# Gathers of an expert's rows issued inside the loop over experts, in three buffers, in place of all in one row before it

## The chip, the cores and the metric

One core of a Trainium2 chip runs the whole program. The metric is device time in microseconds (us) of that core. The engines are TensorE (PE, with its weight loads shown apart as PEld), VectorE (DVE), ScalarE (ACT), GpSimd (POOL) and SyncE (SP); SP issues most DMAs, POOL issues the indirect ones.

## The reference

Linear attention without a softmax, then a mixture of experts in which each token goes to one expert, or to none. There are 8 batches of 576 tokens, 8 heads of 64, so 4608 rows of 512; 8 experts with 512x1024 and 1024x512 weights, all in float32.

```python
kv = einsum('bhsd,bhse->bhde', k, v);  o = einsum('bhsd,bhde->bhse', q, kv)
x = (o / sqrt(mean(o * o, -1) + 1e-6) * g_norm)      # -> (4608, 512)
out = x.copy();  do = x @ w_skip > 0;  xc = x[do]
logits = xc @ w_gate;  e = argmax(logits, 1);  gate = softmax(logits)[e]
for j in range(8):
    rows = (e == j)
    y[rows] = gate[rows] * (relu(xc[rows] @ w1[j]) @ w2[j])
out[do] = xc + y
```

## The kernel before, in words

The first part (to about 142 us of the span) computes attention unit by unit, stores every normalised row x to the output tensor in HBM, and works out for each token its expert and its place within that expert. Experts are taken in the order of how many tokens they have; the r-th of them has room for `CAPS[r]` rows (line 73: 352, 352, 320, 288, 288, 288, 256, 256).

The second part takes the experts one after the other. The rows of an expert are fetched from the output tensor by indirect DMAs on POOL (`gather_piece`, L865, instructions at L868): a "piece" of 128 rows with the index table `src`, and the rest of 64 or 32 rows cut into half or quarter rows, so that 128 partitions are used, with the table `asrc`. An expert has two to four pieces. They lie in a tile `xg`; the tile of expert 0 is `xg0`, and its first piece is fetched early (L682), while attention still runs. `expert_in` (L872) turns a piece with PE transposes (L878) and DVE copies (L881, L883) into `xt`. `layer_1` (L893) makes eight groups of matmuls into PSUM tiles `hps` (L897), each followed by a Relu on ACT (L899) into `ht`; there are three `hps` buffers. `layer_2` (L901) makes the matmuls of one piece into `yps` (L908). `result` (L913) multiplies by the gate and adds x on DVE (L919, in place in `xg`), and scatters the rows back with an indirect DMA on POOL (L922).

The order is written out by hand. Ahead of the loop, `gather_all` (L934, called at L979) issues the 23 pieces that are left, expert 0 first, back to back on POOL. Then come the start of the weights of experts 1 and 2 on SP (`load_ahead`, L980), the sums for the gates, and the second layer of expert 0's first piece. The loop over experts (`experts`, L942) then does for expert r: weights of expert r+2 on SP (L262, L265), `layer_1` of r, `expert_in` of r+1, and for each piece of r `layer_2` and `result`. For expert 0 `first_tables` (L986) runs first: it splits `layer_1` in two halves of four `hps` groups, and after each half PE adds 18 small matmuls for the gates (`place`, L576), whose operand `bv` DVE makes (L567) in one buffer, so that the second `bv` waits until PE has read the first.

```python
for r in range(E):                        # gather_all, L934
    for piece in pieces[r]:
        gather_piece(xgs[r], piece, src, asrc)
```

Gathers read the output tensor and scatters write it. The scheduling layer knows that no two scatters meet, but between a gather and a scatter it puts a wait for whichever stands first in the program. The pools of the second part lie one behind the other in SBUF, over the tiles of the attention part: weights, gathered rows (`gather`), `ffn` (`xt`, `ht`) and `slot` (tables).

After the loop the kernel computes whether any expert had more rows than its room, and repeats the second part in a loop that is not entered with these inputs.

Of the kernel before, what the change touches and what calls it, by code (L numbers as in the profile page):

```python
# [8 lines left out]
FP32 = mybir.dt.float32  # L9
# [8 lines left out]
def kernel(  # L18
# [37 lines left out]
    DM = H * D  # L56
    N = B * S
    P = 128
# [6 lines left out]
    E, F = moe_w1.shape[0], moe_w1.shape[2]  # L65
# [8 lines left out]
    CK = CAP // 128  # L74
# [135 lines left out]
    for a in range(2):  # L210
        r = slice(a * 64, (a + 1) * 64)
# [47 lines left out]
    def load_weights(r, pool):  # L259
        e = experts_of[r]  # L260
        w1 = pool.tile([P, DC, F], FP32, tag="w1", name="w1")
        nc.sync.dma_start(out=w1[:, :, :],  # L262
                          in_=moe_w1[bass.ds(e, 1)].rearrange("o (c p) f -> p (o c) f", p=P))
        w2 = pool.tile([P, FC, DM], FP32, tag="w2", name="w2")
        nc.sync.dma_start(out=w2[:, :, :],  # L265
                          in_=moe_w2[bass.ds(e, 1)].rearrange("o (c p) d -> p (o c) d", p=P))
        w_sb[r] = (w1, w2)
# [385 lines left out]
    xg0 = keep.tile([P, CK, DM], FP32)  # L653
# [120 lines left out]
    with tc.tile_pool(name="wpool_b", bufs=2, reuse_waits="tile") as wpool_b, \  # L774
# [69 lines left out]
        def plan_of(r):  # L844
            pieces = [(c * P, P, r * CK + c) for c in range(CAPS[r] // P)]
            i = 0
            for (_, m), rs in kinds.items():
                for j, (r_, off) in enumerate(rs):
                    if r_ == r:
                        pieces.append((off, m, i + j))  # L850
                i += len(rs)
            return pieces

        plan = [plan_of(r) for r in range(E)]
        whole = [[(c * P, P, r * CK + c) for c in range(CK)] for r in range(E)]
# [9 lines left out]
        def gather_piece(xg, piece, src, asrc):  # L865
            off, m, col = piece
            idx = src if m == P else asrc
            nc.gpsimd.indirect_dma_start(  # L868
                out=x_of(xg, off, m), out_offset=None, in_=cut_rows(m)[:, :],
                in_offset=bass.IndirectOffsetOnAxis(ap=idx[:, col:col + 1], axis=0))  # L870
# [16 lines left out]
        def new_xt():  # L887
            return ffn.tile([P, DC, CAP], FP32, tag="xt", name="xt")

        def new_ht():  # L890
            return ffn.tile([P, FC, CAP], FP32, tag="ht", name="ht")

        def layer_1(r, xt, ht, cols, fs):  # L893
            for f in fs:
                hps = ps_h.tile([P, CAP], FP32, tag="hps", name="hps")
                for dc in range(DC):
                    nc.tensor.matmul(out=hps[:, cols], lhsT=w_sb[r][0][:, dc, f * P:(f + 1) * P],  # L897
                                     rhs=xt[:, dc, cols], start=(dc == 0), stop=(dc == DC - 1))
                nc.scalar.activation(out=ht[:, f, cols], in_=hps[:, cols], func=ACT.Relu)  # L899

        def layer_2(r, ht, piece):  # L901

            off, m, _ = piece
            n = DM * m // P
            yps = ps_y.tile([P, DM], FP32, tag="yps", name="yps")
            for f in range(FC):
                for q in range(P // m):
                    nc.tensor.matmul(out=yps[q * m:(q + 1) * m, 0:n], lhsT=ht[:, f, off:off + m],  # L908
                                     rhs=w_sb[r][1][:, f, q * n:(q + 1) * n],
                                     start=(f == 0), stop=(f == FC - 1), skip_group_check=True)  # L910
            return yps

        def result(piece, yps, xg, tables, group):  # L913

            off, m, col = piece
            n = DM * m // P
            rows, gate = tables[0 if m == P else 1]
            x = x_of(xg, off, m)
            nc.vector.scalar_tensor_tensor(  # L919
                out=x, in0=yps[:, 0:n], scalar=gate[:, col:col + 1], in1=x,  # L920
                op0=ALU.mult, op1=ALU.add)
            ins = nc.gpsimd.indirect_dma_start(  # L922
                out=cut_rows(m)[:, :],
                out_offset=bass.IndirectOffsetOnAxis(ap=rows[:, col:col + 1], axis=0),
                in_=x, in_offset=None, bounds_check=N * P // m - 1, oob_is_err=False)
            tc.declare_no_dep(ins.ins, group=group, reason="each row has one slot")
            tc.add_to_no_dep_group(group, ins.ins)

        def load_ahead(r):
            for ahead in (r, r + 1, r + 2):  # L930
                if ahead < E and ahead not in w_sb:
                    load_weights(ahead, wpool_b if ahead % 3 else wpool_a)

        def gather_all(pieces, src, asrc):  # L934
            xgs = [xg0] + [gather_pool.tile([P, CK, DM], FP32, tag="xg", name="xg", bufs=E - 1)
                           for _ in range(E - 1)]
            for r in range(E):
                for piece in pieces[r]:
                    gather_piece(xgs[r], piece, src, asrc)
            return xgs  # L940

        def experts(pieces, xgs, xt, ht, yps0, tables, group):  # L942

            for r in range(E):
                load_ahead(r)
                todo = pieces[r]
                end = todo[-1][0] + todo[-1][1]
                if r == 0 and yps0 is not None:
                    tables = first_tables(lambda fs: layer_1(r, xt, ht, slice(P, end), fs), tables)
                    result((0, P, 0), yps0, xgs[0], tables, group)  # L950
                else:
                    layer_1(r, xt, ht, slice(0, end), range(FC))
                if r + 1 < E:
                    xt = new_xt()
                    for piece in pieces[r + 1]:
                        expert_in(xgs[r + 1], xt, piece)
                for piece in todo:
                    result(piece, layer_2(r, ht, piece), xgs[r], tables, group)
                del w_sb[r]
                ht = new_ht()  # L960

        first = (0, P, 0)
        assert plan[0][0] == first
        plan[0] = plan[0][1:]
        xt0, ht0 = new_xt(), new_ht()
# [10 lines left out]
        settle(NE, NT, bv)  # L976
        rows, src = slot_rows(slice(0, NCOL), slot_pool, "")
        arows, asrc = again_rows()
        xgs = gather_all(plan, src, asrc)  # L979
        load_ahead(0)  # L980
        gates()
        yps0 = layer_2(0, ht0, first)
# [3 lines left out]
        def first_tables(layer, tables):  # L986

            gp = g_ps[:, GB:GB + 3 * NCOL]
            half = NT // 2
            for i, t in enumerate((0, half)):  # L990
                bv = columns(t, half, colid_i, gate_k, 3, slot_pool, half)
                layer(range(i * FC // 2, (i + 1) * FC // 2))
                place(gp, bv, t, half, t == 0, t == half)
            gate = slot_gates_of(gp)
            agate = slot_pool.tile([P, NRES], FP32, tag="agate", name="agate")
            nc.vector.tensor_copy(out=agate[:, :], in_=again_of(gate))
            return (tables[0], gate), (tables[1], agate)
        experts(plan, xgs, xt0, ht0, yps0, (rows, arows), "first")


        over = slot_pool.tile([P, E, E], FP32)
# [11 lines left out]
        more = slot_pool.tile([P, ROUNDS], FP32)  # L1013
# [10 lines left out]
        with tc.For_i(1, n_rounds, 1):  # L1024
            nc.vector.tensor_single_scalar(out=colid[:, :], in_=colid[:, :], scalar=CK, op=ALU.add)
            nc.vector.tensor_single_scalar(out=number_f[:, :], in_=number_f[:, :],
                                           scalar=float(CAP), op=ALU.add)
            nc.vector.memset(srow[:, :], 0.0)
            add_pieces(srow[:, :], place_all(colid, row_k, 2), 2)

            left = slot_pool.tile([P, NCOL], FP32, tag="left", name="left")
            nc.vector.tensor_tensor(
                out=left[:, :].rearrange("p (r c) -> p r c", c=CK),
                in0=number_f[:, :].unsqueeze(1).to_broadcast([P, E, CK]),
                in1=caps[:, :].unsqueeze(2).to_broadcast([P, E, CK]), op=ALU.is_ge)
            nc.vector.tensor_tensor(out=srow[:, :], in0=srow[:, :], in1=left[:, :], op=ALU.mult)
            rows, src = slot_rows(slice(0, NCOL), slot_pool, "")
            xgs = gather_all(whole, src, None)
            gate = slot_gates(colid)
            xt0 = new_xt()  # L1040
            for piece in whole[0]:
                expert_in(xg0, xt0, piece)
            experts(whole, xgs, xt0, new_ht(), None, ((rows, gate), None), "more")


# [26 lines left out]
```

## Time and profile before

| what | us |
|---|---|
| median of 3 runs | 457.79 |
| lowest and highest run | 456.39, 461.09 |
| the profiled execution | 460.54 |
| its span, first to last instruction | 458.8 |
| mean granted TensorE clock in the span | 0.931 |

All rows are of the one profiled execution; their times count from the start of its span. In a timeline or chain a row gives start, duration and what ran, and in square brackets how long the engine was idle just before and what ended that. "issue" as the releaser means that the profile shows nothing that the engine waited for. In a table by windows each row is one stretch; PEclk is the granted TensorE clock as a share of its upper level of 2.4 GHz, DMA the mean busy share of the 16 DMA engines (overlapping packets can take it over 1), GB/s what they moved.

### The profile page before, as it was taken

The numbers are of one execution on the slowest core, as the hardware profiler recorded it, in microseconds if no ns is written. First come the engines' busy times: TensorE is split into PE (matmuls) and PEld (weight loads), VectorE is DVE, ScalarE is ACT, GpSimd is POOL, SyncE is SP. The second block draws the span as 40 slices with busy tenths as digits, with TensorE's granted clock in tenths as the row PEclk, the third lists the DMA queues.
The fourth block names the chain that finished last, engine by engine and source line by source line (L and its number), as shares of the span: only waits on it lengthen the run. The fifth ranks groups of instructions, "written<-read, shape, count | busy, mean of one in ns | idle before, by whom it ended". The sixth has DMA issues, their size and how long they took to land.

```text
span 458.8 us, 8810 instructions
## 1 busy us (share of the span) xinstructions
PE 389.5 (85%) x3777; PEld 271.7 (59%) x3777; DVE 128.6 (28%) x316; ACT 96.3 (21%) x236; POOL 116.0 (25%) x185
## 2 busy tenths in 40 slices
PE   0699997797655983689999999999999999999980
PEld 0588886676544862455654764674764865856730
DVE  3125566577997630121011010110010011010010
ACT  1156674464531300100210110110110110201100
POOL 2016665545466277102001100100100101001010
PEclk9999998988865997589999999999999999999996
DMA  7999999952379999251541614524623600001000
GB/s 234 332 390 390 397 401 324 338 166 55 94 246 366 356 390 316 85 207 44 179 161 45 221 21 186 161 72 191 193 80 141 211 0 24 25 1 46 0 23 21
DMA packets 32779, 81.82 MB, mean 178 GB/s; under 512 B 3326, under 2 KB 3330, under 8 KB 32736
## 3 DMA queue, kind: packets, MB, share of 16 engines
q1 hardware_dynamic: 26656, 66.59, 41.2%
q0 software_dynamic: 4576, 14.54, 9.0%
q8 instruction: 31, 0.51, 0.5%
q10 hardware_dynamic: 1504, 0.08, 0.2%
q14 instruction: 12, 0.10, 0.1%
HBM read 66.87 MB, written 14.61 MB: 178 GB/s over the span
## 4 chain that ended last, share of the span: by engine, by line
PE 76%; DVE 8%; DMA 7%; issue 5%; ACT 1%; POOL 0%; DVEq 0%; ACTq 0%; POOLq 0%
PE hps L897 30%; PE yps L908 27%; PE o_ps L393 5%; PE sum_ps L291 4%; PE q_ps L353 3%; DMA q<-in_q_dram 2%; DVE xl L422 2%; PE xp L878 2%; DMA xg<-out_dram,src 2%; DMA wraw<-in_moe_w_gate_dram 1%; DMA xg<-out_dram,asrc 1%; PE g_ps L320 1%; DVE oha_k L550 1%; DVE xt L881 1%; DVE rs L405 1%
## 5 line engine op out<-in xcount | busy, mean ns | idle before, releaser
L897 PE MATMUL hps<-xt,w 128*128 128x288 f32 (+5 forms) x576 | 138.4, 400 | 8.4 <-issue 7.6
L908 PE MATMUL yps<-w,ht 128*32 128x128 f32 (+2 forms) x672 | 132.9, 413 | 0.0
L897 PEld LDWEIGHTS hps<-xt,w 128*128 128x128 f32 x576 | 107.7, 198 | 37.9 <-issue 11.9
L908 PEld LDWEIGHTS yps<-w,ht 128*32 128x32 f32 (+2 forms) x672 | 63.8, 145 | 66.1 <-issue 63.1
L899 ACT ACTIVATE ht<-hps 128x288 f32<-128x288 f32 (+5 forms) x72 | 28.3, 393 | 261.1 <-PE hps L897 234.8
L922 POOL DMA_INDIRECT out_dram<-xg,rows x16 | 15.8, 988 | 225.3 <-DVE xg L919 219.4
L919 DVE SCALAR_TENSOR_TENSOR xg<-yps,gate,xg 128x512 f32<-128x512 f32 x16 | 12.0, 751 | 108.5 <-PE yps L908 108.5
L393 PE MATMUL o_ps<-kvn,qT 64*64 64x73 f32 (+1 forms) x384 | 34.1, 271 | 6.5 <-DVE xl L422 5.9
L291 PE MATMUL sum_ps<-v,k 64*64 64x64 f32 x1152 | 26.8, 251 | 14.8 <-DMA v<-in_v_dram 10.5
L881 DVE COPY xt<-xp 128x512 f32<-128x512 f32 x16 | 10.4, 686 | 101.4 <-PE xp L878 97.4
L455 POOL TENSOR_TENSOR xb<-xl,g_b 128x512 f32<-128x512 f32 x32 | 38.3, 1198 | 0.0
L393 PEld LDWEIGHTS o_ps<-kvn,qT 64*64 64x64 f32 (+1 forms) x384 | 28.6, 173 | 14.0 <-DVE xl L422 7.3
L291 PEld LDWEIGHTS sum_ps<-v,k 64*64 64x64 f32 x1152 | 23.7, 162 | 18.1 <-issue 17.3
L393 PE MATMUL o_ps<-kvs,qT 64*64 64x73 f32 (+1 forms) x384 | 33.4, 272 | 0.9 <-issue 0.9
L405 DVE TENSOR_REDUCE rs<-sq 128x8 f32<-128x512 f32 x36 | 24.5, 679 | 16.4 <-ACT sq L397 15.9
L422 DVE TENSOR_TENSOR xl<-o_ps,rs 128x584 f32<-128x584 f32 x36 | 27.6, 767 | 4.7 <-DVE rs L419 0.5
L393 PEld LDWEIGHTS o_ps<-kvs,qT 64*64 64x64 f32 (+1 forms) x384 | 27.9, 173 | 0.4 <-ACT rs L412 0.4
L439 POOL TENSOR_TENSOR lp<-xl 128x36 f32<-128x36 f32 x36 | 9.2, 255 | 68.9 <-DVE xl L422 68.7
L353 PE MATMUL q_ps<-ident,q 128*128 128x128 f32 x128 | 23.4, 312 | 2.8 <-DMA q<-in_q_dram 2.8
L356 ACT COPY qT<-q_ps 128x512 f32<-128x512 f32 x32 | 18.8, 587 | 30.2 <-PE q_ps L353 30.0
L397 ACT ACTIVATE sq<-o_ps 128x512 f32<-128x512 f32 x36 | 21.5, 597 | 15.8 <-PE o_ps L393 15.6
L353 PEld LDWEIGHTS q_ps<-ident,q 128*128 128x128 f32 x128 | 16.2, 157 | 5.6 <-DMA q<-in_q_dram 3.2
(146 smaller groups left out, 243.0 us busy)
## 6 DMA issues: line engine op xcount, KB each, us to landing
w<-in_moe_w_dram SPq DMA_DIRECT2D x16, 2048.0 KB, 8.9
k<-in_k_dram SPq DMA_DIRECT2D x8, 1152.0 KB, 13.1
v<-in_v_dram SPq DMA_DIRECT2D x8, 1152.0 KB, 14.9
q<-in_q_dram SPq DMA_DIRECT2D x8, 1152.0 KB, 13.2
out_dram<-xb SPq DMA_DIRECT2D x8, 512.0 KB, 10.4
out_dram<-xb POOLq DMA_DIRECT2D x8, 512.0 KB
out_dram<-x SPq DMA_DIRECT2D x2, 256.0 KB, 7.9
out_dram<-x POOLq DMA_DIRECT2D x2, 256.0 KB
```

What stands on the lines that cost most here:

```text
L291: nc.tensor.matmul(out=sum_ps[w * 64:(w + 1) * 64, a, u, :], lhsT=kt[r, 2 * u + w, c, :], rhs=vt[r, 2 * u + w, c, :], start=(c == 0), stop ...
L353: nc.tensor.transpose(out=ps[:, w, :, hf, :], in_=qts[b][:, 2 * u + w, c:c + 2, :], identity=ident[:, :])
L356: nc.scalar.copy(out=qT[:, :, :, :].rearrange("p w a t -> p (w a t)"), in_=ps[:, :, :, :, :].rearrange("p w a h t -> p (w a h t)"))
L393: nc.tensor.matmul(out=ps[to, r, cols], lhsT=lhsT, rhs=kv[rows, u, a * KD:(a + 1) * KD], start=True, stop=True, skip_group_check=True)
L397: nc.scalar.activation(out=sq[:, :, :, :], in_=heads(ps, G, G + 2 * D), func=ACT.Square)
L405: nc.vector.tensor_reduce(out=rs[:, :, :], in_=sq[:, :, :, :].rearrange("p r w (a d) -> p r (w a) d", a=2), axis=AX.X, op=ALU.add)
L422: nc.vector.tensor_tensor(out=xl[:, :, :, :].rearrange("p r w (a k) -> p r (w a) k", a=2), in0=ps[:, :, 0:2 * PK].rearrange("p r (h k) -> ...
L455: nc.gpsimd.tensor_tensor(out=xb[:, :, 4 * u * D:(4 * u + 4) * D].rearrange("p r (w x) -> p r w x", w=2), in0=xl[:, :, :, G:G + 2 * D], in ...
L897: nc.tensor.matmul(out=hps[:, cols], lhsT=w_sb[r][0][:, dc, f * P:(f + 1) * P], rhs=xt[:, dc, cols], start=(dc == 0), stop=(dc == DC - 1))
L899: nc.scalar.activation(out=ht[:, f, cols], in_=hps[:, cols], func=ACT.Relu)
L908: nc.tensor.matmul(out=yps[q * m:(q + 1) * m, 0:n], lhsT=ht[:, f, off:off + m], rhs=w_sb[r][1][:, f, q * n:(q + 1) * n], start=(f == 0), s ...
L922: ins = nc.gpsimd.indirect_dma_start(out=cut_rows(m)[:, :], out_offset=bass.IndirectOffsetOnAxis(ap=rows[:, col:col + 1], axis=0), in_=x, ...
```

## The change

`gather_all` now issues the pieces of one expert. Ahead of the loop it is called for experts 0 and 1; in the loop, at the start of the turn of expert r (from r = 1 on), for expert r+1. The tiles of experts 1 to 7 share three buffers in place of seven of their own. The pool is so smaller by four tiles of 3 x 512 floats in each partition (24 KB), and the pools `ffn` and `slot` behind it lie that much lower.

```diff
-        def gather_all(pieces, src, asrc):
-            xgs = [xg0] + [gather_pool.tile([P, CK, DM], FP32, tag="xg", name="xg", bufs=E - 1)
-                           for _ in range(E - 1)]
-            for r in range(E):
+        xgs = {}
+
+        def gather_all(r, pieces, src, asrc):
+            if r < E:
+                xgs[r] = xg0 if r == 0 else gather_pool.tile([P, CK, DM], FP32, tag="xg", name="xg",
+                                                             bufs=3)
                 for piece in pieces[r]:
                     gather_piece(xgs[r], piece, src, asrc)
-            return xgs
...
             for r in range(E):
                 load_ahead(r)
+                if r:
+                    gather_all(r + 1, pieces, *srcs)
                 todo = pieces[r]
...
         arows, asrc = again_rows()
-        xgs = gather_all(plan, src, asrc)
+        for r in range(2):
+            gather_all(r, plan, src, asrc)
         load_ahead(0)
```

On POOL, behind the last gather of expert 1 (its quarter-row piece) and ahead of the first scatter; `xg_211` is the tile of expert 0, and a row "x2" stands for two instructions:

```order
 L868 DMA xg<-out_dram,asrc 128x128
-L868 DMA xg<-out_dram,src 128x512 x2
-L868 DMA xg<-out_dram,asrc 128x256
-L868 DMA xg<-out_dram,src 128x512 x2
-L868 DMA xg<-out_dram,asrc 128x128
-L868 DMA xg<-out_dram,src 128x512 x2
-L868 DMA xg<-out_dram,asrc 128x128
-L868 DMA xg<-out_dram,src 128x512 x2
-L868 DMA xg<-out_dram,asrc 128x128
-L868 DMA xg<-out_dram,src 128x512 x4
 L922 DMA out_dram<-xg_211,rows 4608x512 x2
```

The sixteen gathers of experts 2 to 7 are gone from here (twelve of 128x512, one of 128x256, three of 128x128 floats); seven gathers stay ahead of the first scatter.

On POOL in the changed kernel, from the last scatter of expert 0 to the gathers for expert 3, with what each instruction waits for; `DMASW` names are the semaphores of POOL's DMAs, eight in turn:

```order
L922 DMA out_dram<-xg_211,arows 18432x128 [waits DVE_49]
L868 DMA xg<-out_dram,src 128x512 [waits DMASW6_49,DMASW7_49,DMASW5_49,DMAHW2_49,DMASW4_49,PE_49]
L868 DMA xg<-out_dram,src 128x512
L868 DMA xg<-out_dram,asrc 128x256
L922 DMA out_dram<-xg,rows 4608x512 [waits DMASW1_49,DMASW2_49,DMASW0_49,DVE_49]
L922 DMA out_dram<-xg,rows 4608x512 [waits DVE_49]
L922 DMA out_dram<-xg,arows 9216x256 [waits DVE_49]
L922 DMA out_dram<-xg,arows 18432x128 [waits DVE_49]
L868 DMA xg<-out_dram,src 128x512 [waits DMASW5_49,DMASW6_49,DMASW4_49,DMASW3_49]
L868 DMA xg<-out_dram,src 128x512
L868 DMA xg<-out_dram,asrc 128x128
```

The gathers for an expert now stand behind the scatters of the expert two before it, and the first of them waits until those scatters have landed; the first scatter of the next expert waits until these gathers have landed. PE, DVE, ACT and SP keep the order of their instructions.

## Rows read from the trace of the kernel before

**Rows 1.** The page, busy time, share of the span and instructions of each engine.

```profile
PE 389.5 (85%) x3777; PEld 271.7 (59%) x3777; DVE 128.6 (28%) x316; ACT 96.3 (21%) x236; POOL 116.0 (25%) x185
```

**Rows 2.** The chain that ended last: start us, us, what.

```profile
167.10 6.32 PE hps L897 x32
173.42 0.60 PE g_ps L576 x14
...
174.73 1.93 issue
...
179.47 0.22 PE g_ps L576
...
189.35 0.53 PE hps L897
...
197.16 0.60 PE g_ps L576 x18
...
199.40 0.75 DVE xg L919
...
201.88 13.59 PE yps L908 x112
...
340.39 0.45 PE xp L878 x4
```

**Rows 3.** ACT in order of time, the first three hps groups of expert 0.

```profile
168.92 0.36 ACT L899 ACTIVATE ht<-hps 128x224 f32<-128x224 f32 x1 [10.76 <-PE hps L897]
174.56 0.36 ACT L899 ACTIVATE ht<-hps 128x224 f32<-128x224 f32 x1 [5.28 <-issue]
188.66 0.36 ACT L899 ACTIVATE ht<-hps 128x224 f32<-128x224 f32 x1 [13.75 <-issue]
```

**Rows 4.** DVE in order of time, the second operand for the gates.

```profile
190.32 1.51 DVE L567 TENSOR_TENSOR bv<-ohc,gate_k 128x1296 bf16<-128x1296 bf16 x1 [20.55 <-remote]
```

**Rows 5.** Windows: us, each engine's busy time and instructions, PEclk, DMA share, GB/s.

```profile
160.00:175.00 15.00, 12.89 (x65) 9.29 (x64) 4.92 (x10) 0.72 (x2) 11.50 (x12) 1.00 1.04 389
175.00:180.00 5.00, 0.63 (x3) 0.20 (x2) 0.00 (x0) 0.00 (x0) 3.78 (x4) 0.69 0.99 352
180.00:185.00 5.00, 1.06 (x2) 0.86 (x3) 0.00 (x0) 0.00 (x0) 3.78 (x4) 0.50 0.66 198
185.00:190.00 5.00, 2.13 (x4) 0.86 (x3) 0.00 (x0) 0.36 (x1) 0.95 (x1) 0.50 0.45 144
...
188.50:190.00 1.50, 0.53 (x1) 0.29 (x1) 0.00 (x0) 0.36 (x1) 0.00 (x0) 0.50 0.00 0
...
200.00:205.00 5.00, 4.40 (x10) 1.96 (x9) 2.02 (x5) 0.00 (x0) 1.03 (x1) 0.66 1.01 379
```

**Rows 6.** POOL's gathers and scatters in order of time.

```profile
157.48 1.03 POOL L868 DMA_INDIRECT xg<-out_dram,src  x1 [11.35 <-DVE src L648]
...
166.35 0.94 POOL L868 DMA_INDIRECT xg<-out_dram,src  x1 [0.30 <-issue]
...
185.25 0.95 POOL L868 DMA_INDIRECT xg<-out_dram,src  x1 [0.31 <-issue]
...
244.19 0.98 POOL L922 DMA_INDIRECT out_dram<-xg,rows  x1 [26.63 <-DVE xg L919]
...
256.58 0.98 POOL L922 DMA_INDIRECT out_dram<-xg,arows  x1 [1.20 <-DVE xg L919]
```

**Rows 7.** The chain, what ended the wait for expert 0's last gathered piece.

```profile
160.11 6.12 DMA xg<-out_dram,asrc
```

**Rows 8.** Windows behind the last scatters of experts 1 and 3.

```profile
264.10:272.90 8.80, 8.80 (x35) 6.19 (x34) 0.00 (x0) 1.75 (x4) 0.00 (x0) 1.00 0.00 0
...
325.00:334.60 9.60, 9.60 (x41) 7.55 (x40) 0.35 (x1) 1.64 (x4) 0.98 (x1) 1.00 0.77 249
334.60:340.30 5.70, 5.70 (x25) 4.39 (x25) 0.00 (x0) 1.23 (x3) 0.00 (x0) 1.00 0.00 0
```

**Rows 9.** The page's DMA queues: packets, MB, share of 16 engines.

```profile
q8 instruction: 31, 0.51, 0.5%
```

More of the change, by code (lines that the diff above doesn't have):

```diff
@@ L932, in load_ahead, with experts @@
                     load_weights(ahead, wpool_b if ahead % 3 else wpool_a)
-        def gather_all(pieces, src, asrc):
-            xgs = [xg0] + [gather_pool.tile([P, CK, DM], FP32, tag="xg", name="xg", bufs=E - 1)
-                           for _ in range(E - 1)]
-            for r in range(E):
+        xgs = {}
[3 more added lines that the diff above has]
+                                                             bufs=3)
                 for piece in pieces[r]:
                     gather_piece(xgs[r], piece, src, asrc)
-            return xgs
-        def experts(pieces, xgs, xt, ht, yps0, tables, group):
+        def experts(pieces, srcs, xt, ht, yps0, tables, group):
             for r in range(E):
                 load_ahead(r)
+                if r:
+                    gather_all(r + 1, pieces, *srcs)
                 todo = pieces[r]
@@ L997, in first_tables @@
             return (tables[0], gate), (tables[1], agate)
-        experts(plan, xgs, xt0, ht0, yps0, (rows, arows), "first")
+        experts(plan, (src, asrc), xt0, ht0, yps0, (rows, arows), "first")
         over = slot_pool.tile([P, E, E], FP32)
@@ L1037 @@
             rows, src = slot_rows(slice(0, NCOL), slot_pool, "")
-            xgs = gather_all(whole, src, None)
+            for r in range(2):
+                gather_all(r, whole, src, None)
             gate = slot_gates(colid)
@@ L1042 @@
                 expert_in(xg0, xt0, piece)
-            experts(whole, xgs, xt0, new_ht(), None, ((rows, gate), None), "more")
+            experts(whole, (src, None), xt0, new_ht(), None, ((rows, gate), None), "more")
 _INS = ['q', 'k', 'v', 'g_norm', 'moe_w_skip', 'moe_w_gate', 'moe_w1', 'moe_w2']
```

## The prediction, made before the changed kernel had run

> **What bounds the kernel now.** I read the page first, then the chain of waits in order of time, then ACT, DVE and POOL around the one place where the chain is not PE's own work, and last windows over that place. The page says that PE works for 389.5 us, 85% of the span of 458.8 [rows 1]. So most of the time is matmuls that the change does not touch, and the reader should look for the stretch in which PE does nothing. The chain shows it: after the first half of expert 0's layer 1 (167.10, 6.32 us for 32 records) and 14 of the 18 small gate matmuls, PE goes over to single instructions with gaps of 1 to 2 us put down to "issue", that is, to nothing that the profile shows, and it returns to its usual pace only behind the matmul at 189.35 [rows 2]. From 199.40, when DVE takes the result of expert 0's first piece, the chain is PE's layers up to the end.
>
> I call that stretch the trickle, and these signs go with it. ACT, which waits for nothing but PE there, takes the second hps group at 174.56 and the third at 188.66, though PE had run all four groups by 173.42 [rows 2, 3]. DVE makes the second gate operand at 190.32, over 10 us after the last of the 18 matmuls for which it waits, which ran at 179.47 [rows 2, 4]. So not only are PE's next instructions late, also what PE has done is learnt late by others. The windows tell what runs meanwhile: from 175 to 190 PE is busy for 0.63, 1.06 and 2.13 us of 5, and the granted clock falls to 0.50 [rows 5]. All that time POOL's train of 23 gathers is under way: first at 157.48, then one each 1.25 us, last at 185.25 [rows 6]. In the window 188.50 to 190.00 the DMA engines are quiet (0 GB/s) [rows 5], and just there ACT, PE and DVE come free. I read it so: the trickle belongs to the gathers in flight. It is not plain DMA load: from 160 to 175 the engines moved 389 GB/s at a share of 1.04 and PE was busy for 12.89 us of 15, while from 185 to 190 the share was 0.45 and PE still trickled [rows 5]. Which part of the chip holds PE up I can't read from the trace; that is the weak point of the forecast.
>
> **The change part by part.** Seven gathers stay ahead of the loop (three for expert 0, four for expert 1), the first at 157.48; the row at 166.35 is the first of the sixteen that move [rows 6]. PE ran at its usual pace until 173.4, with ten or more gathers issued [rows 2, 6]. So with seven I expect no trickle.
>
> First term, the trickle. In the traced run 199.40 - 173.42 = 25.98 us pass from the gate matmuls of the first half to DVE's result. Without the trickle this stretch holds: the 18 gate matmuls, 0.60 x 18/14 = 0.77 us; the second half of layer 1, the same work as the first half, 6.32 us; and from 197.16 to 199.40 what stands there now, 2.24 us. Sum 9.33 us [rows 2]. DVE's second operand (1.51 us) lies beside the second half and stays hidden [rows 4]. Gain 25.98 - 9.33 = 16.65 us.
>
> Second term, the clock. The idle PE left the granted clock at 0.66 in the window 200 to 205 [rows 5]. Layer 2 of expert 0's remaining pieces (128, 64 and 32 rows) took 13.59 us [rows 2]; the same three kinds of piece of expert 1 took 256.58 - 244.19 = 12.39 us from scatter to scatter [rows 6]. Gain 1.20 us.
>
> Third term, the sixteen gathers in the loop. POOL's own time there is free: after the train it only scatters, and three issues at 1.25 us, 3.75 us a turn, lie beside PE's layers. What can cost is a gather that lands late, because PE's transposes of expert r+1 stand ahead of layer 2 of r in PE's queue, and everything waits behind them. The chain of a gather is now: last scatter of the expert two before, its landing, two or three issues at 1.25 us, the landing of the last. For the tightest case, r = 4: nothing moves any more from 334.60 on, so the scatters of expert 3 have landed by then [rows 8]; three gathers need 2.5 us to the start of the last and, as the end of the train shows (185.25 to 188.50), at most 3.25 us more [rows 5, 6]. That makes 340.35, and PE wants the rows at 340.39 [rows 2]. So it just fits with the latest landing, and has room if the scatter lands before the load of weights beside it has ended. For r = 2 the quiet begins at 264.10 [rows 8], and with 5.75 us more the rows are there at 269.85, 3 us before the transposes at 272.90. The upper bound is a train of three as it went beside full load, from 157.48 to 160.11 + 6.12 = 166.23, 8.75 us [rows 6, 7]: then r = 4 is 3.0 us late, and r = 2 comes at 272.85, just in time. Doubling the 3.0 for the turns whose rows I don't show, the bounds of this term are 0 and some 6 us of loss; a gain is excluded, since no gather is waited for in the loop now. I take 0.5 us, near the quiet rows, because the loads of weights end before the gathers can begin. A rule speaks against the move: the Trainium skill, page "DMA: Bandwidth & Descriptors", section "Issuing engines are not separate DMA queues", says that transfers issued by different engines share the same 16 DMA engines and interleave, so that a gather on POOL's queue gets no way past the weights on SP's. By it the sum would be the 6 us of loss if both ran together; by the quiet row at 334.60 they hardly meet.
>
> The waits that the lower place of the `xt`, `ht` and table tiles changes concern tiles of the attention part, which ended at 142 us or so; I cost them at nothing, covered by PE's work, and at most at the 1 us that one ACT start could move.
>
> Sum: 16.65 + 1.20 - 0.5 = 17.35 us off the profiled execution's 460.54, which makes 443.2. That execution lies 2.75 us over the median of the three runs, 457.79; taken off the median it would be 440.4. I take 442, about between the two.
>
> **The rivals.** Shorter, not gone: what starves is each engine's fetch of its own instructions, which has to pass the same DMA engines, and the trickle ends when they have room. Then the gain is the bytes that leave the stretch: twelve times 256 KB, once 128 and three times 64 KB, 3.47 MB, at the 389 GB/s of the full stretch 8.9 us [rows 5]. Time 460.54 - 8.9 = 451.6, near 450 against the median. The Trainium skill, page "Runtime: NRT & Kernel Launch", section "Instruction fetch mechanics", says that each sequencer fetches its next block of 16 KiB by a DMA queue of its own while it executes the current one; the trace agrees with 31 packets and 0.51 MB on that queue [rows 9]. For it speaks "issue" as the releaser; against it that the trickle went on at a DMA share of 0.45, and that ACT and DVE were late in seeing PE's finished work, which no fetch of PE explains.
>
> Not touched: the trickle comes from the seven gathers together with the 8 MB of weights of experts 1 and 2, which stay. Then POOL's queue is shorter and nothing else changes: 458. For it speaks that the weights are under way in the first half of the trickle; against it the trickle's last 5 us with a low DMA share, and PE's full pace while the first gathers flew.
>
> Slower: the trickle goes with gathers wherever they are. Then 16.65 us for 23 gathers, or 1.04 each if only the sixteen late ones made it, come back in the loop, where PE is never idle: 16 x 1.04 = 16.7 us, and each of six trains drops the clock for once 1.2 us, 7.2 together. Total 460.54 - 17.85 + 16.7 + 7.2 = 466.6. It is slower than before from (17.85 - 7.2)/16 = 0.67 us a gather. Against it stands that PE ran at pace beside the first nine or ten.
>
> **How the numbers follow.** Trickle gone, 436 to 448 (the two bases, 4 us below for a clock that stays up, the late gathers' 6 us above): 0.58. Shorter, about 450: 0.16. Untouched, about 458: 0.15. Slower, about 466: 0.11. The range runs from 436 up to 458, which leaves out the slow case and half of the untouched one. About 1%, 4.6 us, is what a measurement of this kernel can tell from no change: the first two cases are faster by more, which makes 0.73 with a little taken off for late gathers; the untouched case is the same, 0.16; the last is slower, 0.11.
>
> **What would show it.** Right: on PE no gaps of 1 to 2 us put down to "issue" behind the first half of layer 1; ACT's third hps start some 1.5 us after its second; DVE's result of expert 0's first piece near 183 in place of 199.40; a granted clock that stays at 1.0 (the upper level, 2.4 GHz) from there on; in the loop PE's transposes without a wait for a gather. Wrong: gaps of that kind that last until about 181 (the second case) or 190 (the third), or that turn up behind each train in the loop (the fourth); a wait of PE's transposes for `src` or `asrc` gathers of 2 us and more in several turns would show the third term too small.

## The result, and the profile after

The changed kernel takes 442.53 us (median of 4 runs, 442.13 to 443.48), beside 457.09 us for the kernel before in the same runs (4 runs, 455.11 to 461.09). The ratio is 0.9674, with a 95% interval of 0.9605 to 0.9743: 3.3% faster. (Here and below, medians and ranges are of all runs, while ratios leave out runs that took over 1.5% longer than the fastest of the same kernel.) The profiled execution of the changed kernel took 442.29 us with a span of 440.5 us, 18.3 us less than the span before. So the run fell where the likeliest case had it, 0.5 us from the predicted 442. What the experiments add is that the kernel before does not always show the trickle; where it doesn't, it is as fast as the changed kernel is elsewhere, and there is nothing for the change to take away.

The page of the changed kernel, busy time of each engine (compare [rows 1]):

```profile
PE 381.5 (87%) x3777; PEld 266.7 (61%) x3777; DVE 127.4 (29%) x316; ACT 96.1 (22%) x236; POOL 116.3 (26%) x185
```

The counts are those of before, engine by engine, so no work is gone: what changed is when it runs.

The chain that ended last in the changed kernel, in order of time (start us, us, what), answers to [rows 2]:

```profile
165.56 6.32 PE hps L897 x32
171.88 0.58 PE g_ps L576 x18
172.46 6.13 PE hps L897 x32
...
180.83 0.75 DVE xg L919
...
183.16 14.05 PE yps L908 x112
197.22 19.13 PE hps L897 x64
...
322.15 0.45 PE xp L878 x4
...
427.74 0.75 DVE xg L919
```

The reader should look for what is not there: no "issue" stands between the two halves of layer 1. From the start of the first half to DVE's result of expert 0's first piece, 180.83 - 165.56 = 15.27 us pass, where before it was 199.40 - 167.10 = 32.30 us [rows 2]. That difference, 17.03 us, is nearly the whole result.

ACT of the changed kernel in order of time, the second and third hps groups of expert 0 (compare [rows 3]):

```profile
168.89 0.36 ACT L899 ACTIVATE ht<-hps 128x224 f32<-128x224 f32 x1 [1.16 <-PE hps L897]
170.40 0.36 ACT L899 ACTIVATE ht<-hps 128x224 f32<-128x224 f32 x1 [1.16 <-PE hps L897]
```

The third starts 1.51 us after the second, and what ends ACT's idle time is PE, not "issue". Before, it was 14.1 us.

The windows of the changed kernel over the same place (us, each engine's busy time and instructions, PEclk, DMA share, GB/s; compare [rows 5]):

```profile
175.00:180.00 5.00, 4.30 (x38) 4.08 (x38) 0.54 (x3) 1.07 (x3) 0.00 (x0) 1.00 0.08 21
180.00:185.00 5.00, 4.24 (x20) 2.65 (x21) 2.69 (x6) 0.00 (x0) 1.03 (x1) 0.81 0.97 325
185.00:190.00 5.00, 5.00 (x11) 2.14 (x10) 0.00 (x0) 0.00 (x0) 0.00 (x0) 0.85 0.34 132
```

PE is busy for 4.30 of 5 us from 175 to 180, where it had 0.63. But the granted clock still falls, to 0.81 and 0.85, and that is the first thing that the forecast did not have.

POOL's gathers in the changed kernel in order of time (compare [rows 6]): the last one ahead of the loop, the first two trains in the loop by their first row, and the train of the tightest turn, r = 4, by its first and last row.

```profile
163.97 0.94 POOL L868 DMA_INDIRECT xg<-out_dram,asrc  x1 [0.30 <-issue]
...
205.47 0.99 POOL L868 DMA_INDIRECT xg<-out_dram,src  x1 [6.20 <-DMA out_dram<-xg,arows]
...
245.70 0.99 POOL L868 DMA_INDIRECT xg<-out_dram,src  x1 [6.41 <-DMA out_dram<-xg,arows]
...
316.58 0.99 POOL L868 DMA_INDIRECT xg<-out_dram,src  x1 [7.89 <-PE hps L897]
...
319.15 0.94 POOL L868 DMA_INDIRECT xg<-out_dram,asrc  x1 [0.30 <-issue]
```

And all waits of PE in the changed kernel from 200 to 441 us (engine line waited for: us in total, times, longest us):

```profile
PE xp L878 <- DVE xt L881: 1.4, 4, 0.3
```

POOL waits 6 to 8 us ahead of each of these trains. For the first two the profile names the landing of a scatter, as the new place behind the scatters of the expert two before said it would. For turn 4 it names PE's layer 1 (7.89 us), while in order_only below, with the same order and seven buffers, the wait of that turn (6.05 us) ends with the landing of a scatter; what PE had to release here is not shown. PE waits for no gather at all. In turn 4 the last of three gathers starts at 319.15, and PE begins its transposes at 322.15.

### The profile page after: what moved, and what is told of

It reads as the page before. It is cut to its first block, busy times and chain, and to the rows that moved or that the text cites. A ratio compares the mean times of both kernels' runs of the same rounds, so it can differ in the third digit from the quotient of the medians.

```text
span 440.5 us, 8808 instructions
## 1 busy us (share of the span) xinstructions
PE 381.5 (87%) x3777; PEld 266.7 (61%) x3777; DVE 127.4 (29%) x316; ACT 96.1 (22%) x236; POOL 116.3 (26%) x185
## 4 chain that ended last, share of the span: by engine, by line
PE 74%; DVE 8%; DMA 7%; issue 4%; SPq 1%; ACT 1%; POOL 1%; ACTq 0%; DVEq 0%; POOLq 0%
PE hps L897 30%; PE yps L908 28%; PE o_ps L393 5%; DMA q<-in_q_dram 4%; PE sum_ps L291 3%; PE q_ps L353 2%; DMA wraw<-in_moe_w_skip_dram 2%; DVE xl L422 2%; DMA xg<-out_dram,src 2%; PE xp L878 1%; SPq L105 1%; DVE xt L881 1%; PE g_ps L320 1%; PE g_ps L312 1%; DVE oha_k L550 1%
## 5 line engine op out<-in xcount | busy, mean ns | idle before, releaser
L897 PE MATMUL hps<-xt,w 128*128 128x288 f32 (+5 forms) x576 | 134.7, 395 | 1.2 <-DVE xt L881 0.8
L897 PEld LDWEIGHTS hps<-xt,w 128*128 128x128 f32 x576 | 105.9, 195 | 28.1 <-issue 1.9
L919 DVE SCALAR_TENSOR_TENSOR xg<-yps,gate,xg 128x512 f32<-128x512 f32 x16 | 12.0, 751 | 109.0 <-PE yps L908 109.0
L291 PE MATMUL sum_ps<-v,k 64*64 64x64 f32 x1152 | 24.8, 237 | 13.9 <-DMA v<-in_v_dram 11.1
L291 PEld LDWEIGHTS sum_ps<-v,k 64*64 64x64 f32 x1152 | 21.6, 149 | 17.0 <-issue 16.3
L405 DVE TENSOR_REDUCE rs<-sq 128x8 f32<-128x512 f32 x36 | 24.5, 680 | 18.8 <-ACT sq L397 18.3
L868 POOL DMA_INDIRECT xg<-out_dram,src x15 | 14.7, 977 | 49.4 <-PE hps L897 22.5
```

The source lines that it names most:

```text
L291: nc.tensor.matmul(out=sum_ps[w * 64:(w + 1) * 64, a, u, :], lhsT=kt[r, 2 * u + w, c, :], rhs=vt[r, 2 * u + w, c, :], start=(c == 0), stop ...
L405: nc.vector.tensor_reduce(out=rs[:, :, :], in_=sq[:, :, :, :].rearrange("p r w (a d) -> p r (w a) d", a=2), axis=AX.X, op=ALU.add)
```

## The experiments

The theory (A): the trickle belongs to a long row of gathers that POOL issues back to back, and it goes where the row is cut. The rivals: the DMA engines are full (B); the lower place of the pools made the difference (C). Later one more: the trickle is not always there. The twelve runs were made in four groups; the kernels of a group ran one after the other on one chip, with their own runs of the kernel before.

**Group 1: the kernel before takes 454.87 us here (19 runs, 452.00 to 457.32).**

*order_only.* The changed order, but each expert keeps a tile of its own, so the pools lie as before. Against the changed kernel:

```diff
-                                                             bufs=3)
+                                                             bufs=E - 1)
```

> The changed order of the gathers, but seven buffers as before, so that the ffn and slot tiles lie where they lay before. Theory A (the trickle belongs to a long train of gathers in flight): no trickle, as the changed kernel, 442.5 us. Theory B (it belongs to full DMA engines, and goes with the bytes): also 442.5. Theory C (what helped is the lower place of the ffn and slot tiles, and so other waits): the trickle of before stands, 457.

Measured: 440.61 us (4 runs, 435.98 to 444.35), ratio 0.9656 (0.9574 to 0.9739). The order alone brings the whole gain; the three buffers and the place of the pools bring nothing that shows. In its chain PE's two halves of layer 1 stand 6.90 us apart (164.80 and 171.70), with no trickle.

*place_only.* The order of before, with the pool of gathered rows behind the tables.

```diff
-         tc.tile_pool(name="gather", bufs=1, reuse_waits="tile") as gather_pool, \
          tc.tile_pool(name="ffn", bufs=2, reuse_waits="tile") as ffn, \
          tc.tile_pool(name="slot", bufs=1, reuse_waits="tile") as slot_pool, \
+         tc.tile_pool(name="gather", bufs=1, reuse_waits="tile") as gather_pool, \
```

> The order of before, all 23 gathers in a row, but the pool of gathered rows lies behind the ffn and slot pools, so that those tiles lie low. Theory A and theory B: the trickle stands, ACT's third hps start comes 10 to 15 us after its second, 457 us. Theory C: no trickle, about 443.

Measured: 456.27 us (10 runs), ratio 1.0042 (1.0005 to 1.0079). C falls. The trickle stands here too, and its chain shows one side of it (start us, us, what):

```profile
173.50 2.33 PE hps L897 x8
...
176.21 13.91 another core or an unknown queue
...
190.55 3.31 PE hps L897 x8
```

"remote", or "another core or an unknown queue", is how the profile names a releaser that it doesn't know. DVE and ACT of the same kernel in order of time have the end of it:

```profile
190.05 1.51 DVE L567 TENSOR_TENSOR bv<-ohc,gate_k 128x1296 bf16<-128x1296 bf16 x1 [20.81 <-remote]
190.14 0.85 ACT L899 ACTIVATE ht<-hps 128x224 f32<-128x224 f32 x3 [13.93 <-remote]
```

And PE in order of time has what the chain leaves out:

```profile
173.34 2.14 PE L897 MATMUL hps<-xt,w 128*128 128x224 f32 x10
...
186.46 0.53 PE L897 MATMUL hps<-xt,w 128*128 128x224 f32 x1 [0.89 <-issue]
190.55 3.31 PE L897 MATMUL hps<-xt,w 128*128 128x224 f32 x8 [3.56 <-ACT ht L899]
```

From 175.48 to 186.99 PE trickles as in [rows 2], with gaps of 0.3 to 1.5 us put down to "issue", and gets through what is left of the second and third group of eight matmuls of this half. The first group was done by 175.48, but ACT takes it over 14 us later, at 190.14, and the other two with it in one go. Only from 186.99 on, since the three `hps` buffers are full, does PE wait for ACT. So both signs stand in this run: PE's next matmuls are late, and finished work is learnt late. The last gather of this row starts at 185.99.

*train_in_loop.* Seven gathers ahead of the loop; the other sixteen in one row, at the start of turn 1. Against order_only:

```diff
-                if r:
-                    gather_all(r + 1, pieces, *srcs)
+                if r == 1:
+                    for ahead in range(2, E):
+                        gather_all(ahead, pieces, *srcs)
```

> Seven gathers ahead of the loop and the other sixteen in a row at the start of expert 1's turn, behind expert 0's scatters, with seven buffers. The load of w2 of expert 3 ends there at about 205, when the train starts. Theory A: PE trickles from about the tenth gather of the train (217) until the last lands (227), some 8 to 10 us are lost in layer 1 of expert 1, 451 us. Theory B: the DMA engines are not full beside a train alone, no trickle, 442.5; with so few rows the transposes of expert 2 are not late either.

Measured: 445.56 us (2 runs, 445.32 and 445.80), ratio 0.9808 (0.9761 to 0.9855); by its time between A's 451 and B's 442.5. Its chain through turn 1:

```profile
194.61 19.13 PE hps L897 x64
213.74 0.80 PE xp L878 x4
214.54 2.88 issue
217.42 0.70 DVE xt L881
...
218.85 21.78 PE yps L908 x128
240.63 4.50 PE hps L897 x16
```

POOL's row of gathers beside it, the first and the tenth:

```profile
202.51 0.99 POOL L868 DMA_INDIRECT xg<-out_dram,src  x1 [5.79 <-ACT ht L899]
...
213.85 0.95 POOL L868 DMA_INDIRECT xg<-out_dram,src  x1 [0.30 <-issue]
```

And the windows of this kernel over it:

```profile
215.00:220.00 5.00, 1.83 (x4) 1.16 (x5) 0.69 (x1) 0.03 (x1) 3.77 (x4) 0.70 0.89 311
220.00:225.00 5.00, 5.00 (x8) 1.97 (x7) 1.12 (x2) 0.00 (x0) 1.89 (x2) 0.61 1.02 351
```

Just when the tenth gather of the row has been issued, PE stops for 2.88 us, DVE learns late that the transposes are done, and the granted clock falls to 0.70 and 0.61. From the start of expert 1's layer 1 to that of expert 2's it takes 240.63 - 194.61 = 46.02 us; the changed kernel has 237.23 - 197.22 = 40.01 us there. So a row of sixteen, set 45 us later, brings the same signs with it and costs 6.0 us, of which 2.88 us are the stop and 2.56 us layer 2 at the lower clock (21.78 us beside 19.22 in the changed kernel). A had the mechanism, not the price. PE went from its transposes into layer 2, which waits for no other engine, while in layer 1 it hands over to ACT each 1.5 us; that this is why the row was cheaper here is my reading, and no run isolates it.

*weights_later.* The order of before; the weights of expert 2 take the buffers of expert 0, so that 4 MB less move beside the gathers.

```diff
-                    load_weights(ahead, wpool_b if ahead % 3 else wpool_a)
+                    load_weights(ahead, wpool_b if ahead % 2 else wpool_a)
```

> The order of before, all 23 gathers in a row, but the weights of expert 2 go into expert 0's buffers and so load only from about 180 on, when those come free: 4 MB less beside the gathers. Theory A: the trickle stands until the last gather lands at about 188, 455 to 460 us. Theory B: the engines have room some 10 us earlier, the trickle is short or gone, 443 to 448.

Measured: 454.79 us (8 runs), ratio 1.0012 (0.9977 to 1.0047). The windows of this kernel:

```profile
165.00:170.00 5.00, 4.45 (x23) 4.26 (x24) 3.36 (x6) 0.36 (x1) 4.04 (x4) 1.00 0.46 111
...
180.00:185.00 5.00, 1.89 (x5) 1.07 (x4) 0.00 (x0) 0.36 (x1) 3.79 (x4) 0.50 0.61 168
185.00:190.00 5.00, 2.89 (x6) 1.42 (x6) 0.45 (x1) 0.36 (x2) 0.95 (x1) 0.50 0.45 141
```

The trickle starts at about 173 and stands to 188.71, when PE's chain takes up its pace again. The DMA share is 0.46 just ahead of it and between 0.45 and 0.61 all through it, where the kernel before had 1.04 and 0.99 at its start [rows 5]. B falls: where the engines have near half of their time free, PE still gets 1.89 us of 5.

**Group 2: the kernel before takes 440.36 us here (28 runs, 437.39 to 448.61).** That was the surprise. Here the kernel before is as fast as the changed one elsewhere, and none of the kernels sent here shows the trickle. They were to measure the dose and to part the gathers from their bytes; where there is nothing to remove, they can't.

*ahead_4.* Thirteen gathers ahead of the loop in place of seven (four experts; seven tiles). Against order_only:

```diff
-                    gather_all(r + 1, pieces, *srcs)
+                    gather_all(r + 3, pieces, *srcs)
...
-        for r in range(2):
+        for r in range(4):
             gather_all(r, plan, src, asrc)
```

> Experts 0 to 3 gathered ahead of the loop, 13 gathers in a row in place of 7 or 23, the others two turns ahead; seven buffers. If the trickle begins with about the ninth gather and ends when the last of the train has landed (theory A), it lasts from about 169 to 175: about 2 to 4 us lost, 443 to 446 us. If it needs only a long train as such and 13 is not one, nothing is lost: 441.

Measured: 442.25 us (8 runs), ratio 0.9972 (0.9915 to 1.003).

*bytes_from_sp* and *bytes_from_pool.* Plain DMAs of as many bytes in place of the sixteen gathers, on SP's or on POOL's queue (`nc.sync` or `nc.gpsimd`). They fetch the first rows of the output tensor, so experts 2 to 7 work on those and not on their own (`whole` stands for the repeat that is not entered). Against order_only, for SP:

```diff
+        def fetch_direct(engine, r, pieces):
+            xgs[r] = gather_pool.tile([P, CK, DM], FP32, tag="xg", name="xg", bufs=E - 1)
+            for off, m, _ in pieces[r]:
+                engine.dma_start(out=x_of(xgs[r], off, m), in_=cut_rows(m)[0:P, :])
...
-                if r:
+                if r and pieces is whole:
                     gather_all(r + 1, pieces, *srcs)
...
+        for r in range(2, E):
+            fetch_direct(nc.sync, r, plan)
```

> The same bytes in the same stretch without POOL: experts 2 to 7 take, in place of their own rows, the first rows of the output tensor, fetched by sixteen plain DMAs on SP's queue behind the weights of expert 2; seven gathers stay on POOL. Theory A (gathers on POOL's queue): no trickle, 441. Theory B (full DMA engines): trickle until these transfers end at about 181, some 8 us lost, 450.

> As bytes_from_sp, but the sixteen plain DMAs stand on POOL's queue, in the place of the gathers. If any DMAs of POOL's queue in a long row make the trickle: it stands until they have landed, 450 to 457. If only indirect ones do (an address for each row): no trickle, 441. They read the first rows of the output tensor for experts 2 to 7, so those experts work on other rows.

Measured: 440.30 us (8 runs), ratio 0.9984 (0.993 to 1.0037), and 441.40 us (8 runs), ratio 1.0023 (0.9985 to 1.006).

*spaced.* The order of before, with two additions of zeros on POOL ahead of each of the last sixteen gathers, so that they start 3.3 us apart in place of 1.25:

```diff
+            pause = xgs[E - 1][:, CK - 1, :]
+            if pieces is plan:
+                nc.gpsimd.memset(pause, 0.0)
             for r in range(E):
                 for piece in pieces[r]:
+                    if pieces is plan and r > 1:
+                        for _ in range(2):
+                            nc.gpsimd.tensor_tensor(out=pause, in0=pause, in1=pause, op=ALU.add)
                     gather_piece(xgs[r], piece, src, asrc)
```

> The order of before, all 23 gathers ahead of the loop, but two additions of 128x512 zeros on POOL (about 1.2 us each) ahead of each of the last sixteen, so that they start some 3.7 us apart and each has landed before the next starts; the train ends at about 225, and the scatters of expert 0 stand behind it. If several gathers in flight make the trickle: none, 441 to 444. If the count of gathers or the work on POOL makes it: trickle from the ninth gather until 225, with PE slow in layer 2 of expert 0 and layer 1 of expert 1 too, 465 or more.

Measured: 441.88 us (8 runs), ratio 1.0051 (1.0006 to 1.0095). None of these four differs from the kernel before by more than some 0.5%, and no theory is told from another by them; what they had to tell stays open. Nor do they show that the additions of spaced cost anything: the same kernel comes out at 0.9995 in group 3.

**Group 3: the kernel before takes 441.15 us here (15 runs, 437.75 to 447.15).** Two kernels ran again: the unchanged kernel before, for a profile of its own, and the spaced one.

> The kernel before, unchanged, to see its trace beside the runs of one chip: with the four kernels sent together last, it took 440 us where it had taken 455 and 457. If that chip knows no trickle at all, a chip on which it takes 440 shows ACT's four hps starts 1.5 us apart and PE without gaps put down to issue beside all 23 gathers; a chip on which it takes 455 shows the trickle as traced first, 14 us or so from ACT's second to its third start.

> The kernel of spaced once more. On a chip on which before takes about 455: if several gathers in flight make the trickle, none here and 441 us; if the number of gathers or POOL's work on them makes it, a trickle from the ninth gather on to about 220, 465 us or more. On a chip on which before takes about 440 it tells nothing, 441.

Measured: 441.02 us (8 runs, ratio 0.9996, 0.9941 to 1.005) and 440.38 us (8 runs, ratio 0.9995, 0.994 to 1.0051). There was no trickle again, so spaced_again says nothing, but before_again is what shows that the trickle itself is missing. POOL of the unchanged kernel before in this run, the first and the last of its 23 gathers:

```profile
154.86 1.03 POOL L868 DMA_INDIRECT xg<-out_dram,src  x1 [10.63 <-DVE src L648]
...
183.81 0.94 POOL L868 DMA_INDIRECT xg<-out_dram,src  x1 [0.30 <-issue]
```

Its chain:

```profile
164.21 6.32 PE hps L897 x32
...
171.11 6.13 PE hps L897 x32
...
179.49 0.75 DVE xg L919
...
181.82 12.36 PE yps L908 x112
194.18 19.13 PE hps L897 x64
```

And two of its windows:

```profile
160.00:175.00 15.00, 14.18 (x83) 12.04 (x82) 5.58 (x8) 2.14 (x6) 11.68 (x11) 1.00 1.03 387
175.00:180.00 5.00, 4.30 (x43) 4.08 (x43) 1.14 (x5) 0.72 (x2) 3.79 (x4) 1.00 0.96 334
```

The row is as long and as dense as in [rows 6], the DMA share as high as in [rows 5] (1.03 beside 1.04, 0.96 beside 0.99), and PE goes through its halves as if nothing were there: 15.28 us from the first half to L919, where the changed kernel has 15.27. So the row of gathers and the load on the DMA engines don't suffice for the trickle; something of the chip, or of its condition at that time, has to come with them.

**Group 4: the kernel before takes 456.50 us here (11 runs, 454.52 to 466.73).** The trickle's time is back; of the kernel before there is no trace from this group, only its time. The record gives groups 3 and 4 the same chip number, 0, and they ran less than five minutes apart, at 441.15 and 456.50 us. If that number stands for one and the same chip, the level is not a property of the chip but of its condition at the time; the record doesn't say whether it does.

> The changed kernel, unchanged. On a chip on which before takes about 440 (no trickle there, as the trace of before_again showed): the change has nothing left to take away and the gathers in the loop cost nothing, so the two are the same within 1%, ratio 0.99 to 1.01. If the late gathers have a price of their own that the trickle's end has hidden so far, it shows here alone: up to 1.01 to 1.015. On a chip on which before takes about 455: 0.965 to 0.97 again.

> The kernel of spaced a third time. On a chip on which before takes about 455: several gathers in flight as the cause, no trickle and 441; their number or POOL's work on them as the cause, a trickle from the ninth gather to about 220 and 465 or more. On a chip on which before takes about 440: 441, and nothing told.

Measured: after_again, the changed kernel once more, 440.54 us (6 runs), ratio 0.9644 (0.9598 to 0.969); spaced_third 441.84 us (4 runs, 440.82 to 442.72), ratio 0.9673 (0.9616 to 0.9729). POOL of spaced_third in order of time, two gathers with the additions between them, and the last gather:

```profile
174.86 0.96 POOL L868 DMA_INDIRECT xg<-out_dram,asrc  x1 [0.15 <-issue]
175.84 2.17 POOL L944 TENSOR_TENSOR xg<-xg 128x512 f32<-128x512 f32 x2
178.15 0.96 POOL L868 DMA_INDIRECT xg<-out_dram,src  x1
...
217.64 0.96 POOL L868 DMA_INDIRECT xg<-out_dram,src  x1
```

Its chain over the place of the trickle:

```profile
163.97 6.32 PE hps L897 x32
...
170.88 6.13 PE hps L897 x32
...
179.25 0.75 DVE xg L919
...
181.58 14.05 PE yps L908 x112
```

All 23 gathers stand ahead of the loop again, in the order of before, and POOL is at them until 218 us; yet the trickle is gone, and with it as much time as the change saves. So where the kernel before has the trickle's time, neither the number of gathers nor their place ahead of the loop makes it; it takes a row without pauses. Whether the pauses do it, or that fewer gathers are in flight at once, this run does not part.

## Why the prediction was right, and where it was not

**First term, the trickle: right.** Worked out were 9.33 us from the gate matmuls of the first half to DVE's result; measured are 180.83 - 171.88 = 8.95 us. The gain was to be 16.65 us and is 25.98 - 8.95 = 17.03 us. The signs named ahead came one by one: no issue gaps, ACT 1.51 us apart, L919 at 180.83 (named: near 183). The reason, that seven gathers are too few, is borne out by the cut row (order_only) and by the row moved with its trickle (train_in_loop); the spaced one adds that the number alone does not make it. What the prediction held to be enough, "gathers in flight", is not: before_again had as many.

**Second term, the clock: failed.** The prediction took it that the granted clock fell because PE was idle, and that it would stay at 1.0 without the trickle, giving 1.20 us. Expert 0's remaining layer 2 took 14.05 us, 0.46 us more than the 13.59 us of before [rows 2], at a granted clock of 0.81 and 0.85, though PE had been busy for 4.30 of the 5 us ahead. In before_again, with the same 4.30, the clock stayed up and the same matmuls took 12.36 us; in order_only too (12.36), in spaced_third not (14.05), in after_again 13.51. The other half of the reason fails as well: in place_only and weights_later PE had trickled at a granted clock of 0.50, as in the kernel before, and the same matmuls took 12.36 us right after it. So this term is 1.2 to 1.7 us that come or don't, with the trickle or without; it was no part of the change.

**Third term, the gathers in the loop: mis-sized, 0 in place of 0.5 us.** From the end of expert 0's layer 2 to the transposes of turn 4 it took 340.39 - 215.47 = 124.92 us before (215.47 being 201.88 + 13.59, [rows 2]); after, 322.15 - 197.21 = 124.94 us. No turn lost anything. For turn 4 the prediction had the third gather start at 334.60 + 2.5 = 337.10, 3.29 us ahead of the transposes; measured are 322.15 - 319.15 = 3.00 us. The room was as small as thought, and it was enough; the rows of that third gather themselves are transposed last, at 323.37, 4.22 us behind its start, which the forecast had not reckoned with. Of the loss that was worked out beside the rule of the Trainium skill on shared DMA engines (page "DMA: Bandwidth & Descriptors", section "Issuing engines are not separate DMA queues") nothing shows: the loads and the gathers hardly met. In the changed kernel the DMA share is 0.98 from 200 to 205 and 0.46 from 205 to 210, and the first train starts at 205.47.

**Not foreseen: 1.54 us upstream.** The first half of layer 1 starts at 165.56 in place of 167.10. The change does not touch what comes before, and 1.14 us of it already stand at the first of the gathers (156.34 in place of 157.48). The unchanged kernel itself had the first half at 164.21 in before_again, and the changed one at 163.83 in after_again, so it is the spread of what comes before from run to run. It stood in for the missing second term: 17.03 + 1.54, less 0.32 between L919 and expert 1's layer 1 (16.39 us after, 16.07 before), make 18.25 of the 18.3 us by which the spans differ. The forecast's 17.35 for the traced pair had the right size partly by errors that cancel.

**The rivals.** "Shorter, not gone" fell with weights_later: the trickle stays where the DMA engines are half free. "Untouched" fell with the result. "Slower" was right about one half: the trickle does go along with a long row into the loop, at 6.0/16 = 0.38 us a gather, under the 0.67 us from which the change would have lost; with two or three in a row, and 40 us from the first train in the loop to the second, it never appears. What no text of mine had is a fifth case: a chip, or a time, at which the kernel before has no trickle. There the change has nothing to win. It was not run beside before there; that it would cost nothing is likely, since ahead_4, which has its later gathers in the loop too, was no slower there than before (0.9972), and since from the start of expert 1's layer 1 to the last L919 it takes 427.74 - 197.22 = 230.52 us, and before_again 424.70 - 194.18 = 230.52 us, but it is not shown.

**Still open.** What in the chip holds back the news of finished work; why it does so in some places and not in others; how many gathers in a row it takes (PE's own gaps began behind the tenth in train_in_loop, and when fourteen or fifteen had been issued in the rows of before and place_only; there ACT was late earlier, with the second group due at about 170.4 in before, 1.5 us behind the first, when eleven had been issued, and taken at 174.56 [rows 3]); whether plain DMAs on POOL would do the same. Group 2 was to tell the last two, where it could not. All runs on record come with a span and a granted clock, and so from under the profiler; whether the trickle stands without it is open too. None of the kernels beats the changed one by more than its interval: order_only, after_again and spaced_third lie between 440.5 and 441.9 us.

## What to carry to other kernels

Where an engine stands idle with a releaser that had long been done, or with "issue", look for what else was dense at that time, on engines that have nothing to do with it: here, at some times, a row of 23 indirect DMAs on POOL, 1.25 us apart, held up ACT and DVE by 14 us and more, and PE with them, and cutting the row or spacing it to 3.3 us ended that. Have gathers issued a few at a time, just ahead of their use, when there is room for it in the queue; that cost nothing in this loop. And take the time of the kernel before in several places and at several times before an edit is credited with a gain: the same program took 457 us in one and 441 us in another, as far apart as the edit is worth.

## What the runs showed of the hardware that was not expected

- The same kernel has two levels that differ by about 3.4%: 454.87 and 456.50 us in groups 1 and 4 (30 runs, none under 452.00), 440.36 and 441.15 us in groups 2 and 3 (43 runs, none over 448.61). Within a group it never changed. Groups 3 and 4, on different levels, have the same chip number on record. Of the 21.3 us between the two traced spans (458.8 and 437.5) the trickle makes 32.30 - 15.28 = 17.02.
- Finished work can be learnt over 14 us late: a group of matmuls that PE had done by 175.48 is taken by ACT at 190.14, in one go with two later ones, and DVE's second gate operand starts at 190.05, though the gate matmuls for which it waits had ended at 173.50 (place_only).
- The granted clock fell to 0.81, 0.85 (after) or 0.66 (spaced_third, window 180 to 185) where PE was as busy as in runs in which it stayed at 1.00 (before_again, order_only; 4.24 of 5 us in all four).

The last point rests on these rows, the window from 180 to 185, first of spaced_third:

```profile
180.00:185.00 5.00, 4.24 (x9) 1.89 (x9) 1.85 (x5) 0.00 (x0) 4.53 (x6) 0.66 1.02 417
```

and of before_again:

```profile
180.00:185.00 5.00, 4.24 (x14) 1.95 (x13) 2.09 (x5) 0.00 (x0) 3.79 (x4) 1.00 1.06 360
```

The busy time of PE and the DMA share are nearly the same in both, the clock is not; which of the two a run gets can't be read from what precedes it in these rows.
